# Spreading the FFT units of each batch evenly over its period, with seven products from an earlier group on

## Chip, cores and metric

The kernel runs on one core of a Trainium2 chip. The metric is the device time of one execution in microseconds (us). The kernel before takes 782.4 us (median of the first three executions).

## The reference, cut to what matters

```python
# x: (8, 3008, 256) float32; n_freq = 1505
X = np.fft.rfft(x, axis=1)
y = np.fft.irfft(X * (filt_r + 1j * filt_i)[None], n=3008, axis=1)   # filter along the sequence
x = y.reshape(8 * 3008, 256)
h = np.maximum(x @ w_in, 0.0)                                        # 256 -> 2048
out = h * h @ w_out                                                  # 2048 -> 256
```

Eight batches are filtered, then all 24064 rows go through a feed-forward layer. The kernel overlaps the two: while TensorE works on the feed-forward layer of one batch, the Fourier transform of the next is done in between.

## The kernel before

Time is cut into slots. Group `g` of 512 rows has 8 slots. In each slot TensorE computes two of the 16 hidden blocks of group `g` (L553, four matmuls of 512 columns) and one part of the second layer of group `g-1`. That second layer is either 64 matmuls of 256 columns (L573) or, from group 9 on, seven products of half size (a Strassen-like scheme, 112 matmuls of 128 columns, L666), for which VectorE forms four sums and does three additions.

FFT units of a batch are put between these parts, at "place" 0 (after the first layer's part) or place 1 (after the second layer's) of a slot:

- A, forward: x16 to PSUM, evicted into `u`, which goes to DRAM (`dU`). 16 units.
- read_u: `dU` back as `ut`, 1.5 MB in a different order.
- B, filter: PSUM times the filter on VectorE into `prod`; GpSimd issues two DMAs that add its halves. 12 units.
- P, inverse: from `prod` to PSUM, evicted into `ze`, which goes to DRAM (`dZ`). 12 units.
- read_z: `dZ` back as `zt`. Y, inverse: `zt` to PSUM, evicted into `yt`, the rows of the first layer. 16 units.

All of A, B, P and Y use the same two PSUM banks, and A, Y and P are evicted by ScalarE or VectorE behind whatever else these have in their queues:

```python
def psF(name):
    return pps.tile([128, 512], F32, tag="psF", name=name, bufs=2)
...
def unit_a(b, a):
    ...                                   # one or two matmuls into psF
    if a % 2 == 0: nc.scalar.copy(out=o, in_=pv)
    else:          nc.vector.tensor_copy(out=o, in_=pv)
    if i == 3:     write_u(b, c)          # nc.sync.dma_start
def read_u(b):
    ut = p_ut.tile([128, NC, D], F16, ...)               # one buffer
    for s0, s1 in ((0, 8), (8, 24)):                     # 512 KB, 1024 KB
        nc.sync.dma_start(out=ut[:, s0:s1, :], in_=v[:, s0:s1, :])
def unit_b(b, p):
    ...                                   # two matmuls into psF
    nc.vector.tensor_mul(out=prod, in0=ps..., in1=sF...)
    for i in range(2): nc.gpsimd.dma_start(..., accum_op=add)
def unit_p(b, p):                         # two matmuls into psF, nc.scalar.copy
    ...
def fft_plan(b):                          # r: slot in the batch's frame of 48 slots
    ...
    t0 = 2 if b == 1 else 5
    for a in range(12 if b == 1 else 0, 16): put(t0 + a // 2, a % 2, unit_a, b, a)
    put(10 if b == 1 else 13, 1, read_u, b)
    t0 = 14 if b == 1 else 18
    for p in range(12):
        r = t0 + (15 if b == 1 else 18) * p // 11
        put(r, 0, unit_b, b, p)
        ...
        put(r + 4, 1, unit_p, b, p)
    t0 = 34 if b == 1 else 41
    for c in range(4): put(t0 if c < 3 else t0 + 6, 1, read_z, b, c)
    for n in range(16): put((38 if b == 1 else 45) + n // 2, n % 2, unit_y, b, n)
...
for s in range((NG + 1) * SLOTS):
    g, k = divmod(s, SLOTS)
    ffn_g1(g, k)                          # matmuls, then relu on ScalarE
    run(work, s, 0)                       # FFT units of place 0
    products(...) or ffn_g2(g - 1, k)     # second layer of the group before
    run(work, s, 1)                       # FFT units of place 1
    ffn_out / sums(g - 1, k); ffn_sq(g, k)
```

(The guards on `g` and the prologue, which does batch 0 and half of batch 1, are left out.)

## Time and profile before

| | before |
|---|---|
| time, median of 3 | 782.36 us |
| span of the profiled run | 780.7 us |
| matmuls at their usual pace | 745.7 us |
| holes on TensorE, whole span | 28.2 us |
| of these after 60 us | 18.4 us |

A "hole" here is the time from one matmul's start to the next, less the median of that distance for the first one's shape, where over 0.1 us is left. It is used instead of the idle times in the profile because a matmul's end is modelled there. The prediction below shows the lines of the page, the waits, the windows and the timeline on which this rests, and how each is read.

### The profile page before, as it was taken

The page shows a single profiled execution, that of the slowest core. Times are in us where ns is not written, and L with a number is a line of the kernel's source. Part 1 is how long each engine was busy: PE and PEld are TensorE (multiplying, and loading weights), DVE is VectorE, ACT ScalarE, POOL GpSimd, SP SyncE. Part 2 cuts the span into 40 slices and gives each one's busy share as a digit, 9 for nine tenths or more (in the row PEclk, how much of TensorE's full clock was granted, in tenths as well). Part 3 has the DMA queues.
Part 4 walks back from the last instruction along what each step waited for, and adds up shares of the span by engine and source line. Part 5 has one row for each costly group of instructions (what it writes and reads, how often), then busy time and mean ns, then how long its engine had stood idle before and what let it go on. Part 6 is the DMA issues. An engine that isn't in the chain of part 4 may idle for free. (4 is left out here: it accounts for less than half of the span.)

```text
span 780.7 us, 18857 instructions
## 1 busy us (share of the span) xinstructions
PE 755.4 (97%) x7878; PEld 552.5 (71%) x7878; DVE 627.2 (80%) x699; ACT 561.6 (72%) x785; POOL 193.0 (25%) x260
## 2 busy tenths in 40 slices
PE   8989999999999999999999999999999999999998
PEld 6746667667676676876778767777767767777776
DVE  6856644567778997899978999899988999987874
ACT  3976776767777677776777777776777767777774
POOL 3801730036100561005500065002840035100000
PEclk9999999999999999999999999999999999999999
DMA  9985974369534795167953578525875355521011
GB/s 365 375 253 160 149 161 116 89 158 175 136 80 119 169 171 145 57 180 130 171 116 96 173 127 149 154 76 158 149 145 126 89 151 128 128 78 55 29 55 55
DMA packets 104941, 109.20 MB, mean 140 GB/s; under 512 B 9640, under 2 KB 93096, under 8 KB 102936
## 3 DMA queue, kind: packets, MB, share of 16 engines
q1 hardware_dynamic: 85704, 87.38, 37.3%
q0 software_dynamic: 19008, 20.43, 19.5%
q8 instruction: 62, 1.02, 0.6%
q10 hardware_dynamic: 144, 0.18, 0.1%
q14 instruction: 23, 0.19, 0.1%
HBM read 58.12 MB, written 48.23 MB: 136 GB/s over the span
## 5 line engine op out<-in xcount | busy, mean ns | idle before, releaser
L557 ACT ACTIVATE h<-psH 128x1024 f16<-128x1024 f32 x376 | 384.6, 1024 | 172.2 <-PE psH L553 170.3
L553 PE MATMUL psH<-yt,sWin 128*128 128x512 f16 (+7 forms) x1728 | 386.9, 351 | 1.5 <-DVE yt L532 0.5
L564 DVE TENSOR_TENSOR h<-h 128x2048 f16<-128x2048 f16 (+1 forms) x192 | 229.6, 1196 | 64.8 <-ACT h L557 64.3
L457 POOL DMA_DIRECT2D prod<-prod x168 | 141.1, 997 | 463.7 <-DVE prod L450 458.4
L553 PEld LDWEIGHTS <-sWin 128*128 128x128 f16 x1728 | 153.4, 98 | 98.5 <-issue 3.4
L666 PEld LDWEIGHTS <-sum 128*128 128x128 f16 x2368 | 146.8, 98 | 27.2 <-issue 6.1
L666 PEld LDWEIGHTS <-h 128*128 128x128 f16 x1776 | 110.3, 98 | 22.5
L450 DVE TENSOR_TENSOR prod<-psB,sF 128x1024 f16<-128x1024 f32 x84 | 102.4, 1219 | 14.4 <-PE psB L442 14.4
L666 PE MATMUL psX<-sT,sum 128*128 128x128 f16 x1184 | 84.2, 219 | 0.0
L573 PE MATMUL psO<-sWout,h 128*128 128x256 f16 x640 | 81.8, 272 | 0.0
L573 PEld LDWEIGHTS <-h 128*128 128x128 f16 x640 | 62.0, 98 | 14.6 <-issue 0.2
L532 DVE CAST yt<-psY 128x376 f16<-128x376 f32 x62 | 33.8, 546 | 34.4 <-PE psY L523 34.4
L489 ACT CAST ze<-psP 128x512 f16<-128x512 f32 x84 | 49.4, 588 | 13.4 <-PE psP L487 8.9
L666 PE MATMUL psY<-sT,sum 128*128 128x128 f16 x592 | 57.2, 219 | 0.0
L666 PE MATMUL psY<-sWout,sum 128*128 128x128 f16 x592 | 44.9, 219 | 5.5 <-DVE bot L681 5.5
L364 DVE CAST u<-psA 96x512 f16<-96x512 f32 x50 | 34.1, 683 | 17.1 <-PE psA L358 14.9
L523 PE MATMUL psY<-sC,zt 112*128 112x94 f16 x512 | 42.4, 205 | 5.1 <-DMA zt<-dZ 4.9
L195 POOL DMA_DIRECT2D x<-in_x_dram x40 | 46.1, 1151 | 0.0
L642 DVE TENSOR_TENSOR sum<-sum,h 128x2048 f16<-128x2048 f16 x37 | 45.2, 1221 | 0.9
L666 PE MATMUL psY<-sWout,h 128*128 128x128 f16 x592 | 45.2, 219 | 0.0
L666 PE MATMUL psX<-sT,h 128*128 128x128 f16 x592 | 45.1, 219 | 0.0
L639 DVE TENSOR_TENSOR sum<-h 128x2048 f16<-128x2048 f16 x37 | 44.9, 1215 | 0.1
(88 smaller groups left out, 706.0 us busy)
## 6 DMA issues: line engine op xcount, KB each, us to landing
zt<-dZ SPq DMA_DIRECT2D x64, 192.0 KB
dU<-u SPq DMA_DIRECT2D x28, 384.0 KB
prod<-prod POOLq DMA_DIRECT2D x168, 64.0 KB, 3.6
dZ<-ze SPq DMA_DIRECT2D x28, 384.0 KB
x<-in_x_dram POOLq DMA_DIRECT2D x40, 192.0 KB, 5.3
ut<-dU SPq DMA_DIRECT2D x7, 1024.0 KB
xw<-in_x_dram SPq DMA_DIRECT2D x6, 1024.0 KB
ut<-dU SPq DMA_DIRECT2D x7, 512.0 KB
```

Source lines behind the costliest of these rows:

```text
L195: nc.gpsimd.dma_start(out=t, in_=v[:, m, :])
L450: nc.vector.tensor_mul(out=prod, in0=ps.rearrange("p (a d) -> p a d", d=D).unsqueeze(1).to_broadcast([128, 2, 2, D]), in1=sF[:, :, 2 * p:2 ...
L457: nc.gpsimd.dma_start(out=prod[64 * i:64 * i + 64, 0], in_=prod[64 - 64 * i:128 - 64 * i, 1], accum_op=mybir.AluOpType.add)
L489: nc.scalar.copy(out=zes[(b, c)][:, 2 * i6:2 * i6 + 2, :], in_=ps.rearrange("p (a d) -> p a d", d=D))
L523: nc.tensor.matmul(ps[:, 94 * jj:94 * jj + 94], zt[:, 4 * (g % 2) + jj, dt * 128:(dt + 1) * 128], sSY, start=True, stop=True)
L553: nc.tensor.matmul(ps[:, i, o:o + n], sWin[:, dt, jt * 128:(jt + 1) * 128], yts[b][:, dt, r:r + n], start=(dt == 0), stop=(dt == 1))
L557: nc.scalar.activation(out=h2[:, 2 * s:2 * s + 2, :], in_=ps, func=AF.Relu)
L564: nc.vector.tensor_mul(out=v, in0=v, in1=v)
L573: nc.tensor.matmul(pso[g][:, t % 2, :], h2s[g][:, jt, t * 128:(t + 1) * 128], sWout[:, jt, :], start=(jt == 0), stop=(jt == NJT - 1))
L639: nc.vector.tensor_add(out=t, in0=a21, in1=a22)
L642: nc.vector.tensor_sub(out=t, in0=f[5], in1=a11)
L666: nc.tensor.matmul(o[:, t, :], f[p][:, q, 128 * t:128 * t + 128], sg["w"][p][:, q, :], start=(m == 0 and p in (1, 2)), stop=(q == 7), skip ...
```

## The change

Its intent: take the bursts away. Filter units come every 3.5 slots in place of 1.6, forward units every 2.75 in place of two per slot; the odd forward evictions move from VectorE to ScalarE; the last P unit is two slots earlier so that z has time to come back; and the cheaper seven-product form starts at group 6.

```diff
-    p_prod = ... bufs=4
+    p_prod = ... bufs=5
-        if a % 2 == 0:
+        if a % 2 == 0 or b > 2:
             nc.scalar.copy(out=o, in_=pv)
-    ztiles = [... for c in range(3)]
+    ztiles = [... for c in range(2)]
@@ fft_plan: put(r, f, *a) now takes r in half slots
-        t0 = 2 if b == 1 else 5
-        for a in range(12 if b == 1 else 0, 16):
-            put(t0 + a // 2, a % 2, unit_a, b, a)
-        put(10 if b == 1 else 13, 1, read_u, b)
+        else:
+            for a in range(16):
+                if a % 2 == 0 and b > 2:
+                    put((-57 + 2.3 * a) if b == 3 else (-66 + 2.75 * a), load_x, b, a // 2)
+                put((-16 + a, -46 + 2.2 * a, -56 + 2.75 * a)[min(b, 4) - 2], unit_a, b, a)
+            put(2 if b == 2 else -9, read_u, b)
-            r = t0 + (15 if b == 1 else 18) * p // 11
-            put(r, 0, unit_b, b, p)
-            put(r + 4, 1, unit_p, b, p)
+            r = 14 + 15 * p / 11 if b == 1 else 6 + 28 * p / 11 if b == 2 else -5 + 39 * p / 11
+            put(r, unit_b, b, p)
+            put(r + 4.5, unit_p, b, p)
-        for c in range(4):
-            put(t0 if c < 3 else t0 + 6, 1, read_z, b, c)
-        for n in range(16):
-            put((38 if b == 1 else 45) + n // 2, n % 2, unit_y, b, n)
+        for c in range(4):
+            put((41, 41.5, 48, 54)[c] - d, read_z, b, c)
+        for n in range(16):
+            put(YN[n] - d, unit_y, b, n)
+    YN = (45, 45.5, 46, 46.5, 47.5, 49, 50.5, 52, 54, 56, 58, 60, 63, 66, 69, 72)
-    SEVEN = range(9, NG - 1)
+    SEVEN = range(6, NG - 1)
```

(Cut: the four operand differences of the seven products go to four slots in place of one, and the last read of z of batch 0 is placed later.)

More of the change, by code (lines that the diff above doesn't have):

```diff
@@ L143 @@
     p_ut = ctx.enter_context(tc.tile_pool(name="p_ut", bufs=1))
-    p_prod = ctx.enter_context(tc.tile_pool(name="p_prod", bufs=4))
+    p_prod = ctx.enter_context(tc.tile_pool(name="p_prod", bufs=5))
     p_ze = ctx.enter_context(tc.tile_pool(name="p_ze", bufs=3))
@@ L494, in unit_p @@
                 in_=zes.pop((b, c)))
-    ztiles = [const.tile([112, 8, D], F16, name=f"zt_{c}") for c in range(3)]
+    ztiles = [const.tile([112, 8, D], F16, name=f"zt_{c}") for c in range(2)]
     for t in ztiles:
@@ L501, in read_z @@
     def read_z(b, c, ks=(0, 1)):
-        zt = ztiles[c % 3]
+        zt = ztiles[c % 2]
         v = dZ[b].rearrange("(q j) d -> q j d", j=NM)
@@ L609, with make_t @@
     sg = {}
-    def make_t():
-        t = p_t.tile([128, 4, 8, 128], F16, tag="t", name="sT")
+    def make_t(k):
         w = sWout.rearrange("p (q e) c -> p q e c", e=2)
@@ L616, in make_t @@
         b21, b22 = w[:, :, 1, 0:128], w[:, :, 1, 128:256]
-        nc.vector.tensor_sub(out=t[:, 0], in0=b12, in1=b11)
-        nc.vector.tensor_sub(out=t[:, 1], in0=b22, in1=t[:, 0])
-        nc.vector.tensor_sub(out=t[:, 2], in0=b22, in1=b12)
-        nc.vector.tensor_sub(out=t[:, 3], in0=b21, in1=t[:, 1])
+        if k == 0:
+            sg["t"] = p_t.tile([128, 4, 8, 128], F16, tag="t", name="sT")
+        t = sg["t"]
+        i0, i1 = ((b12, b11), (b22, t[:, 0]), (b22, b12), (b21, t[:, 1]))[k]
+        nc.vector.tensor_sub(out=t[:, k], in0=i0, in1=i1)
         sg["w"] = {1: b11, 2: b21, 3: b22, 4: t[:, 3], 5: t[:, 0], 6: t[:, 1], 7: t[:, 2]}
@@ L692, in fft_plan, with put @@
         plan = {}
-        def put(r, place, f, *a):
-            plan.setdefault((r, place), []).append((f, a))
+        def put(r, f, *a):
+            r = int(2 * r)
+            plan.setdefault(divmod(r, 2), []).append((f, a))
+        d = 0
         if b == 1:
             for n in range(4, 16):
-                put(n if n < 8 else n + 2 if n < 12 else 2 * n - 7, n % 2, unit_y, 0, n)
+                put((n if n < 8 else n + 2 if n < 12 else 2 * n - 7) + n % 2 / 2, unit_y, 0, n)
+            put(7.5, read_z, 0, 3)
             for k in range(4):
-                put((4, 5, 7, 7)[k], 1, cast_wout, k, nc.vector)
-        t0 = 2 if b == 1 else 5
-        for a in range(12 if b == 1 else 0, 16):
-            put(t0 + a // 2, a % 2, unit_a, b, a)
-        put(10 if b == 1 else 13, 1, read_u, b)
-        t0 = 14 if b == 1 else 18
-        for p in range(12):
-            r = t0 + (15 if b == 1 else 18) * p // 11
-            put(r, 0, unit_b, b, p)
-            if b + 1 < B and 2 <= p < 10:
-                put(r, 0, load_x, b + 1, p - 2)
-            put(r + 4, 1, unit_p, b, p)
-        t0 = 34 if b == 1 else 41
+                put((4.5, 5.5, 7.5, 7.5)[k], cast_wout, k, nc.vector)
+            for a in range(12, 16):
+                put(2 + a / 2, unit_a, b, a)
+            put(10.5, read_u, b)
+            d = 7
+        else:
[4 more added lines that the diff above has]
+            put(2 if b == 2 else -9, read_u, b)
+        for p in range(12):
+            r = 14 + 15 * p / 11 if b == 1 else 6 + 28 * p / 11 if b == 2 else -5 + 39 * p / 11
+            put(r, unit_b, b, p)
+            if b == 1 and 2 <= p < 10:
+                put(r, load_x, 2, p - 2)
+            put(r + 4.5, unit_p, b, p)
         for c in range(4):
-            put(t0 if c < 3 else t0 + 6, 1, read_z, b, c)
+            put((41, 41.5, 48, 54)[c] - d, read_z, b, c)
         for n in range(16):
-            put((38 if b == 1 else 45) + n // 2, n % 2, unit_y, b, n)
+            put(YN[n] - d, unit_y, b, n)
         return plan
+    YN = (45, 45.5, 46, 46.5, 47.5, 49, 50.5, 52, 54, 56, 58, 60, 63, 66, 69, 72)
     def run(plan, r, place):
@@ L791 @@
     prologue[0] = False
-    for c in range(2, 4):
-        read_z(0, c)
-    SEVEN = range(9, NG - 1)
+    read_z(0, 2)
+    SEVEN = range(6, NG - 1)
     work = {}
@@ L806 @@
         run(work, s, 0)
-        if s == SEVEN[0] * SLOTS:
-            make_t()
+        if SEVEN[0] * SLOTS <= s < SEVEN[0] * SLOTS + 4:
+            make_t(s % SLOTS)
         if (s - 1) // SLOTS - 1 in SEVEN:
```

## The prediction

> **What bounds the kernel now.** I read the page first, then the waits, then the batches window by window, then the timeline at the holes.
>
> ```profile
> span 780.7 us, 18857 instructions
> ...
> PE 755.4 (97%) x7878; PEld 552.5 (71%) x7878; DVE 627.2 (80%) x699; ACT 561.6 (72%) x785; POOL 193.0 (25%) x260
> ...
> DVE  6856644567778997899978999899988999987874
> ```
>
> TensorE is the bound, and its clock row is full throughout. VectorE averages 80% but has slices at 9: its bursts. The page overstates PE, because a matmul's end is modelled. So I took start-to-start times from the timeline: the usual pace is 0.216 us for 512 columns, 0.109 for 256, 0.056 for 128, 0.041 for a 94-column inverse matmul. All matmuls at these paces come to 745.7 us; what exceeds a pace by over 0.1 us I call a hole. Holes sum to 28.2 us, of which 18.4 lie after 60 us (the rest is the prologue and the first slots, which the change hardly touches). These 18.4 us are all that a reordering can win.
>
> Who ends them, in the waits view:
>
> ```profile
> PE psY L666 <- DVE bot L681: 5.5, 5, 1.2
> PE psY L523 <- DMA zt<-dZ: 4.9, 7, 1.4
> ...
> PE psP L487 <- DMA prod<-prod: 2.6, 4, 0.7
> ```
>
> These are idle times counted from the modelled ends, so they are low. By my starts, after 60 us: accumulator additions by VectorE 6.8 us (a hole of 1.3 to 1.4 and one of 0.12 in each of five batches); z arriving late 4.4 (six holes, 0.37 to 1.06); products of the inverse arriving late, late in the burst, 4.1; u arriving late 0.8; waits for a psF bank 1.6; others 0.7. The batches repeat:
>
> ```profile
> core 0: us, PE busy (x) PEld busy (x) DVE busy (x) ACT busy (x) POOL busy (x), PEclk, DMA share, GB/s
> ...
> 308.30:402.30 94.00, 91.14 (x1026) 68.08 (x1024) 84.09 (x95) 69.16 (x100) 24.07 (x32) 1.00 0.61 137
> ...
> 717.66:730.82 13.16, 13.16 (x147) 9.39 (x145) 10.45 (x12) 9.35 (x12) 0.00 (x0) 1.00 0.13 41
> ```
>
> A batch takes 94.0 us, 90.5 of it matmuls at pace; the tail's groups, with no FFT beside them, run without a hole at 13.16 us. The largest hole, as timeline:
>
> ```profile
> 264.04 0.39 PE L666 MATMUL psY<-sWout,h 128*128 128x128 f16 x4
> ...
> 264.61 1.21 DVE L564 TENSOR_TENSOR h<-h 128x2048 f16<-128x2048 f16 x1
> ...
> 265.74 1.21 DVE L450 TENSOR_TENSOR prod<-psB,sF 128x1024 f16<-128x1024 f32 x1
> ...
> 266.88 0.41 DVE L681 TENSOR_TENSOR top<-psY,top 128x256 f32<-128x256 f32 x1
> ...
> 267.21 0.41 DVE L681 TENSOR_TENSOR bot<-psY,bot 128x256 f32<-128x256 f32 x1
> ...
> 267.67 0.38 PE L666 MATMUL psY<-sWout,sum 128*128 128x128 f16 x4 [1.24 <-DVE bot L681]
> ```
>
> The addition's input is complete at 264.3, but VectorE first works off a square and a filter product queued ahead, and TensorE stands until the addition has read the bank. This is burst damage: filter units every 1.6 slots.
>
> **What the Trainium skill says.** "TensorE: Matmul & The Clock Gate", "Wait — 56ns, not 53.3ns?", puts a warm matmul at N/2.4 GHz plus about 2.5 ns; the chain's 16 matmuls of 128 columns in 0.89 us (0.0556 each) agree. The same page, "Back-to-back issue gap", gives about 81 ns for N=128 with a weight load each; this trace has a weight load each and holds 0.056, so the measurement decides (with 81 the seven-product form would lose). "PSUM — Partial Sum Buffer", "Engine vs sequencer instructions", says the ScalarE and VectorE queues are strict FIFO; the fence above is that. "VectorE: DVE Perf Modes", "The perf-mode tier table", gives 1224 ns for a 2048-element bf16 tensor_tensor and the slowest mode with a PSUM operand: here 1.196 us for 2048 and 1.219 us for 1024 from PSUM.
>
> **The change part by part.**
> 1. Seven products from group 6 instead of 9: three groups trade 64 matmuls of 256 columns (8 in 0.88 us, so about 7.0) for 112 of 128 columns (112 x 0.056 = 6.3). 0.7 to 0.8 us each, on the path: -2.3 us. VectorE gets 3 x (4 x 1.216 + 3 x 0.417) = +18.3 us, at 150 to 200 us where it was half idle. The four operand differences (0.68 us each) go to four slots.
> 2. The odd forward evictions of batches 3 to 7 go to ScalarE: 40 x 0.683 = -27.3 us of VectorE, 40 x 0.573 = +22.9 us of ScalarE. Totals: VectorE about 618, ScalarE about 586. Neither becomes the bound on average.
> 3. Filter units now every 3.5 slots in place of 1.6, with no forward evictions on VectorE. In the burst VectorE had 11.0 (four squares, four sums, three additions) / 8 + 1.22 / 1.64 = 2.1 us per slot against some 1.9 of TensorE; now 1.37 + 0.34 = 1.7. The addition holes should go: -6.4 of 6.8. The fifth product buffer and the quieter GpSimd queue should remove the late products, -4.0.
> 4. The last inverse-side product moves from slot 40.5 of the batch's frame to 38.5 while z is still used at 45. Each earlier slot is 1.9 us, the largest hole 1.06: -3.4 for batches 2 to 7 (batch 1 keeps its distance and its 1.0). u is read 4 slots ahead, but its writes now end before the read instead of just ahead of it: -0.7.
> Sum of 3 and 4: -14.5. No matmul is added.
>
> **What comes back.** All FFT units share two psF banks, so a unit waits for the eviction of the unit two before it. Before, dense phases had one unit per half slot, ScalarE and VectorE taking turns, and lost nothing to speak of. Where three units fell within half a slot the trace shows a price:
>
> ```profile
> 136.50 1.02 ACT L557 ACTIVATE h<-psH 128x1024 f16<-128x1024 f32 x1 [0.70 <-PE psH L553]
> ...
> 137.42 0.47 ACT L530 CAST yt<-psY 128x376 f16<-128x376 f32 x1
> ...
> 137.94 0.33 PE L523 MATMUL psY<-sC,zt 112*128 112x94 f16 x4 [0.21 <-ACT yt L530]
> ```
>
> The eviction stands behind the 1.02 us relu: 0.38 us lost by starts, then 0.32 by the next unit, and 0.44 twice (84 and 93 us) behind a filter product. Listing both plans by slot and half slot, the old has 8 such triples, the new 45, because four streams (forward A, filter B, inverse P, inverse Y) of different spacing now cross: 20 in slots 19 to 71, where batches 1 to 3 meet, six in each of the next four batch frames, one in the last. Worst is three at one place (P, B, A in slot 29): the third wants a bank whose eviction has not begun: relu 0.92 + copy 0.58 less 0.22 of matmuls, some 1.2 us. Working through the triples with 0.92 us of relu, 0.35 to 0.58 of copy, 1.22 of filter product: about 7 us in the early stretch (1.6 of it existed), 1.5 in each of four batches, 0.6 in the last; 12 more than before. Stalls let the evictors catch up, so one prevents the next: I take 9.
>
> Net: -2.3 - 14.5 + 9.0 = -7.8 us. 782.4 - 7.8 = **774.6 us**.
>
> **Rivals.** (a) Spreading works as meant: ScalarE's slack within a slot (1.02 of relu in 1.9) absorbs the crossings. For: Y and A ran at two units a slot before without loss, and the spacings look hand-picked. New holes 2 to 3 us: about 768. (b) The two banks become the wait in place of the additions, at full count or more, because a filter product on VectorE holds a bank until the sums ahead of it are done: 14 to 16 us of new holes, 780 to 782. For: the measured 0.3 to 0.4 per triple and strict FIFO. Against: the old triples on ScalarE alone often cost nothing. (c) VectorE stays the bound locally, where sevens, filter units and inverse evictions now coincide (150 to 200 us: about 1.9 us a slot against 1.95): addition holes of about 1 us survive in group 6 to 9, 1 to 3 us on top of any of these. (d) Transfers: DMA share falls in the peaks (0.97 to 0.99 before) as traffic spreads; I expect no new wait on one.
>
> **Range and chances.** With no hole left at all after 60 us: 782.4 - 2.3 - 18.4 = 761.7, a floor. (a) at 768 and (b) at 781 bound the likely outcomes: low 765.5, high 780.5. Faster by over 2% needs under 766.7, more than (a) delivers: 0.12. Slower needs new holes of over 30 us: 0.01. Within 2%: 0.87.
>
> **What would show it.** Right: the wait of TensorE for the bottom addition falls from 5.5 us to under 1; waits for z from 4.9 to about 2.5 (the prologue's and batch 1's remain); for products to under 1; VectorE's digits in the middle are flatter. New rows should be waits of forward, filter and inverse matmuls on ScalarE's u, ze, yt copies and on the filter product, 8 to 12 us together by starts, most before 200 us. Batches 4 to 6 should take 91.5 to 92.5 us in place of 94. Wrong: a batch still at 93.5 or more, holes ended by a transfer, or ScalarE's relus late so that the first layer's matmuls wait (0.5 us before).

## More of the kernel before

Unless a run is called slow, every number here is from executions in the fast state. The sets ran on several chips; each ratio is to the kernel before in the same set, and holes are read from one profiled execution per version.

## The result, and the profile after

The changed kernel takes 787.16 us (785.37 to 787.64, 4 runs) against 783.03 us of the kernel before in the same rounds. The ratio is 1.0052, with a 95% interval of 1.0027 to 1.0077: slower by half a per cent. (All ratios are the mean time of one kernel's fast runs over that of the other's of the same rounds, so not quite the ratio of the medians quoted.)

The page of the changed kernel, in the rows that answer to those shown in the prediction:

```profile
span 785.6 us, 19161 instructions
...
PE 756.2 (96%) x8022; PEld 554.5 (71%) x8022; DVE 619.7 (79%) x679; ACT 583.7 (74%) x831; POOL 192.7 (25%) x260
...
DVE  5866655579768988888987899779987999878874
```

VectorE and ScalarE moved as intended (627.2 to 619.7 and 561.6 to 583.7 us), and VectorE's row has fewer nines. Yet the span grew by 4.9 us. The waits of TensorE:

```profile
PE psY L523 <- DMA zt<-dZ: 6.8, 4, 2.5
...
PE psP L487 <- DVE prod L450: 3.0, 7, 0.5
...
PE psA L358 <- DVE prod L450: 2.8, 11, 0.3
...
PE psY L523 <- ACT h L557: 2.3, 2, 1.2
...
PE psA L358 <- ACT ze L489: 1.5, 2, 1.1
```

The columns are total, times and longest. The wait for the bottom addition (5.5 us before) and the one for a product's DMA (2.6) are gone from the list. The wait for z has grown from 4.9 to 6.8, with a longest of 2.5 in place of 1.4, and A and P units now wait for evictions. By starts, after 60 us, and by what the stopped unit needed:

| holes after 60 us, us | before | after |
|---|---|---|
| bottom addition (L681) late | 6.9 | 0 |
| product of B late for P | 4.1 | 0 |
| u late for B | 0.8 | 0 |
| z late for the first Y | 4.5 | 8.9 |
| psF bank not yet evicted | 1.6 | 14.5 |
| others | 0.5 | 0.8 |
| sum | 18.3 | 24.2 |

(The sum before is 18.35, hence 18.3 here and 18.4 above.) With this, the 4.9 us are accounted for: matmuls at pace 745.7 to 743.6, that is -2.1; holes after 60 us +5.9; excesses of under 0.1 us from 0.5 to 1.8, that is +1.3; prologue -0.2. Two new losses thus have to be explained, z and psF.

**The z holes.** One stretch around the largest, from the timeline of the changed kernel, of SyncE's queue (SPq: start and duration of the issues) and of the units concerned:

```profile
211.08 0.58 ACT L489 CAST ze<-psP 128x512 f16<-128x512 f32 x1
...
211.69 0.38 SPq L492 DMA_DIRECT2D dZ<-ze  x1
...
212.18 1.83 SPq L433 DMA_DIRECT2D ut<-dU  x2
...
214.11 1.65 SPq L606 DMA_DIRECT2D out_dram<-bot  x3
...
215.86 1.34 SPq L606 DMA_DIRECT2D out_dram<-top  x3
...
218.22 3.77 SPq L505 DMA_DIRECT2D zt<-dZ  x4
...
224.81 0.47 PE L523 MATMUL psY<-sC,zt 112*128 112x94 f16 x4 [2.52 <-DMA zt<-dZ]
```

The last P unit is evicted at 211.7, so the intended lead is there. But right behind its write to DRAM stands the read of u, 1.5 MB, for the next batch. The read of z is issued at 218.2 only. The list of SyncE's waits has the reason:

```profile
SPq L505 <- DMA ut<-dU: 11.7, 7, 2.3
```

L505 is the read of z. In the program's order a transfer waits for the one eight before it on this queue (they share a completion semaphore), and in batch 2 that is the read of u. In batches 3 to 6 the two reads that the first Y needs did not wait for u; the next two did, and the other waits of the line are theirs. There z's first reads were issued in time but did not move in time: in batch 3 the first was issued at 311.8, but in the trace's list of packets the 4096-byte packets of z begin at 316.5, after u's and behind the stores issued between (in the four batches 4.2 to 4.8 us after the issue); the matmul starts at 319.7. So both kinds of waiting are there: for the completion of u once, for its bytes in the queue four times. In the kernel before, u is read at slot 13 of the frame and z at 41, so they never meet. Batches 2 to 6 have such holes (2.7, 1.3, 1.6, 1.3 and 2.0 us). Batch 7, after which no u is read, has none.

The 2.7 us hole also costs clock. Windows of the changed kernel around it (PEclk is the granted clock, the share of full speed that TensorE was given):

```profile
core 0: us, PE busy (x) PEld busy (x) DVE busy (x) ACT busy (x) POOL busy (x), PEclk, DMA share, GB/s
...
223.00:225.00 2.00, 0.19 (x3) 0.22 (x4) 0.00 (x0) 0.35 (x1) 0.09 (x1) 0.87 1.13 213
225.00:226.00 1.00, 1.00 (x13) 1.00 (x11) 0.00 (x0) 0.47 (x1) 0.00 (x0) 0.50 1.21 168
226.00:227.00 1.00, 1.00 (x12) 1.00 (x10) 0.00 (x0) 0.00 (x0) 0.00 (x0) 0.50 0.45 86
227.00:228.00 1.00, 1.00 (x8) 0.62 (x7) 0.44 (x1) 0.39 (x2) 0.00 (x0) 0.56 0.02 4
```

For some 3 us TensorE runs at half pace (the trace's record of the clock has 0.5 from 224.5 to 227.9). After 60 us, the traces have such a stretch in four versions, each at a hole of 2.1 us or more or within 1.2 us of its end (2.1, 2.5, 2.7 and 4.3 us), and at no hole of up to 2.0 us. The +1.3 us of small excesses fit that: matmuls of 128 columns at twice 0.056 us stay under the 0.1 us from which I count a hole.

**The psF holes.** One of the worst, from the timeline of the changed kernel at slot 29, where P, B and A stand at one place:

```profile
107.43 0.38 PE L487 MATMUL psP<-prod,sSP 128*128 128x256 f16 x2
107.63 1.02 ACT L557 ACTIVATE h<-psH 128x1024 f16<-128x1024 f32 x1 [0.59 <-PE psH L553]
107.65 0.38 PE L442 MATMUL psB<-ut,sSB 128*128 128x256 f16 x2
...
108.56 0.58 ACT L489 CAST ze<-psP 128x512 f16<-128x512 f32 x1
...
109.19 0.38 PE L358 MATMUL psA<-x,sC 94*96 94x512 f16 x1 [1.15 <-ACT ze L489]
```

P takes one bank, B the other, and A wants P's bank at 107.9. ScalarE first does the slot's relu, then evicts P at 108.6 to 109.1. TensorE stands 1.3 us by starts.

### The profile page after: what moved, and what is told of

The parts are those of the page before. It is cut to its first block, busy times and chain, and to the rows that moved or that the text cites.

```text
span 785.6 us, 19161 instructions
## 1 busy us (share of the span) xinstructions
PE 756.2 (96%) x8022; PEld 554.5 (71%) x8022; DVE 619.7 (79%) x679; ACT 583.7 (74%) x831; POOL 192.7 (25%) x260
## 4 chain that ended last, share of the span: by engine, by line
PE 82%; DMA 7%; DVE 6%; ACT 2%; issue 1%; SPq 1%; DVEq 0%; ACTq 0%
PE psH L553 36%; PE psX L666 17%; PE psY L666 12%; PE psO L573 6%; DVE prod L450 3%; PE psA L358 3%; PE psP L487 2%; PE psY L523 2%; DMA zt<-dZ 2%; PE psB L442 2%; DMA f<-in_filt_i_dram 2%; ACT h L557 1%; DVE h L564 1%; DMA ut<-dU 1%; DVE sum L639 1%
## 5 line engine op out<-in xcount | busy, mean ns | idle before, releaser
L666 PEld LDWEIGHTS <-sum 128*128 128x128 f16 x2560 | 158.9, 98 | 25.2 <-issue 1.4
L666 PEld LDWEIGHTS <-h 128*128 128x128 f16 x1920 | 119.1, 98 | 20.5 <-issue 1.4
L666 PE MATMUL psX<-sT,sum 128*128 128x128 f16 x1280 | 91.9, 220 | 0.0
L666 PE MATMUL psY<-sT,sum 128*128 128x128 f16 x640 | 62.0, 219 | 0.0
L573 PE MATMUL psO<-sWout,h 128*128 128x256 f16 x448 | 56.9, 272 | 0.0
L523 PEld LDWEIGHTS <-zt 112*128 112x128 f16 x512 | 34.3, 98 | 29.1 <-issue 10.4
L362 ACT CAST u<-psA 96x512 f16<-96x512 f32 x90 | 52.3, 581 | 2.8 <-PE psA L358 2.2
L573 PEld LDWEIGHTS <-h 128*128 128x128 f16 x448 | 43.2, 98 | 14.8 <-issue 4.5
L642 DVE TENSOR_TENSOR sum<-sum,h 128x2048 f16<-128x2048 f16 x40 | 48.9, 1222 | 0.9
L648 DVE TENSOR_TENSOR sum<-h,sum 128x2048 f16<-128x2048 f16 x40 | 48.7, 1216 | 0.0
L639 DVE TENSOR_TENSOR sum<-h 128x2048 f16<-128x2048 f16 x40 | 48.6, 1216 | 0.0
```

The source lines that it names most:

```text
L523: nc.tensor.matmul(ps[:, 94 * jj:94 * jj + 94], zt[:, 4 * (g % 2) + jj, dt * 128:(dt + 1) * 128], sSY, start=True, stop=True)
L573: nc.tensor.matmul(pso[g][:, t % 2, :], h2s[g][:, jt, t * 128:(t + 1) * 128], sWout[:, jt, :], start=(jt == 0), stop=(jt == NJT - 1))
L639: nc.vector.tensor_add(out=t, in0=a21, in1=a22)
L642: nc.vector.tensor_sub(out=t, in0=f[5], in1=a11)
L666: nc.tensor.matmul(o[:, t, :], f[p][:, q, 128 * t:128 * t + 128], sg["w"][p][:, q, :], start=(m == 0 and p in (1, 2)), stop=(q == 7), skip ...
```

## The experiments

Four questions: are the psF triples the cause of the psF holes; is the read of u the cause of the z holes; what is each remaining part of the change worth; and do the cures add up?

### Seven products alone

The kernel before with `SEVEN = range(6, NG - 1)` and the operand differences spread over four slots.

> The kernel before with only the seven products from group 6 (and the four operand differences in four slots). By pace 3 x (64 x 0.109 - 112 x 0.056) = 2.1 us less, about 781 if VectorE has room in groups 6 to 8. If VectorE's 18 us of added sums between 150 and 200 us make new holes, 783 or more.

Measured: 782.14 us, ratio 1.000 (0.998 to 1.002). The 2.1 us of pace are there (743.6), but holes on the bottom addition went from 6.9 to 8.9 us, and one product came 1.8 us late at 199 us. A new addition hole of 1.4 us stands at 172.6 us, so in the bursts of the old plan VectorE had no room for 18 us more in groups 6 to 8. In this trace holes after 60 us grew by 1.0 us in all, half of the gain; the times of the set show none of it, within some 1.6 us.

### No three psF users within a slot

```diff
+    # no three units of the two psF banks within one slot: Y and A units step aside
+    for fs in ((unit_b, unit_p), (unit_y,), (unit_a,)):
+        ...
+                while count.get(t, 0) + max(count.get(t - 1, 0), count.get(t + 1, 0)) > 1:
+                    t += 1      # half a slot later
```

B and P stay where the changed kernel has them. No matmul, eviction or transfer is added or taken away.

> The changed kernel with forward and inverse units moved by half slots, most by 0.5 to 1.5 and in batch 2 up to 5, so that no three units that use the two psF banks fall within one slot; nothing else. Theory B (the triples make the new holes, each third unit waiting for an eviction behind a relu or a filter product): psF holes fall from about 14.5 us to under 4, time 10 us less, about 777. Rival V (those holes come from VectorE and ScalarE being too full on average once three groups more use sevens and ScalarE has all forward evictions): moving units by half slots keeps over 10 us of them, time over 784. The z holes (8.9 us) stay.

Measured: 774.23 us, ratio 0.9905 (0.9877 to 0.9933); 787.16 to 774.23 is 13 us (the two sets ran apart; by their ratios it is 11.5). psF holes fell from 14.5 to 0.8 us and z holes stayed at 8.2. So the engines were not too full: the crossings of the four streams made the holes.

### The read of u earlier

```diff
-            put(2 if b == 2 else -9, read_u, b)
+            put(2 if b == 2 else -11.5, read_u, b)
```

> The changed kernel with one edit: from batch 3 on the read of u is put 2.5 slots earlier (at -11.5 in place of -9), so that its 1.5 MB are through before z is read. Theory Q (the read of u for the next batch now stands just ahead of the read of z in the same DMA queue and holds it back): the five z holes of batches 2 to 6 (8.9 us by starts in the changed kernel) shrink to under 3 us in all, time 6 us less than the changed kernel, about 781. Rival T (z is late because its own write to DRAM and read back are slow however early they are issued): holes stay within 1 us of 8.9, time unchanged at 787. The psF holes (14 us) stay in both.

Measured: 792.91 us (787.92 to 794.86), ratio 1.0121 (1.0092 to 1.0150): the expected time was wrong. The z holes did shrink, from 8.9 to 1.3 us, as theory Q wants. But u now meets the last product of the batch. The timeline of this run:

```profile
579.28 1.64 POOL L457 DMA_DIRECT2D prod<-prod  x2 [6.33 <-DVE prod L450]
...
579.84 0.81 SPq L433 DMA_DIRECT2D ut<-dU  x2
...
588.75 0.61 PE L487 MATMUL psP<-prod,sSP 128*128 128x256 f16 x2 [4.14 <-DMA prod<-prod]
```

GpSimd issues the two DMAs that add the halves of the product just as u's read begins. The second took 8.9 us to land, against a median of 2.8. Holes on products came to 7.4 us in four batches, where there were none. The profiled run is the fastest of the six (787.9), so the others lost more than its trace shows; their granted clocks are 0.989 to 0.998, where it has 0.998 with one stretch of half clock behind the 4.3 us hole. The wait had only moved.

### The read of u through another queue

```diff
-            nc.sync.dma_start(out=ut[:, s0:s1, :], in_=v[:, s0:s1, :])
+            (nc.gpsimd if b > 2 else nc.sync).dma_start(out=ut[:, s0:s1, :], in_=v[:, s0:s1, :])
```

> The changed kernel with one edit: from batch 3 on the same read of u, at the same place, is issued by GpSimd's queue in place of SyncE's. The bytes in flight are the same; only the order within SyncE's queue changes, where a transfer waits for the one eight before it. Theory Q1 (it is the place in the queue: z's read is issued only when u's read, 8 or 9 issues before, has landed): z holes fall from 8.9 to under 3 us, time about 781. Theory Q2 (it is the bandwidth that 1.5 MB of u take while z is read): z holes stay over 6 us, time within 2 us of 787.

Measured: 780.05 us, ratio 0.9972 (0.9955 to 0.9988). z holes 1.7 us, psF holes 15.1 as before. That agrees with Q1 in the numbers, but the run does not separate Q1 from Q2. GpSimd's queue was not held up by the write of z, so u's read began at 300.5 in batch 3, 4.6 us ahead of that write in place of 0.5 us behind it, and its last packet had ended (309.4) when z was read (309.6). One product came 0.5 us late. What it shows is that z is in time once u is not in front of it.

### u in pieces on the same queue

(Shortened.)

```diff
-                put(-9, read_u, b)                       # 512 KB and 1024 KB
+                for k in range(4):
+                    put(-9 + 10.5 * k, read_u, b, k)     # 384 KB each, 3 filter units' worth
```

> The changed kernel with one edit: from batch 3 on u is read in four pieces of 384 KB, 10.5 slots apart, on SyncE's queue as before, the first at the same place. Theory Q (1.5 MB of u between z's write and z's read hold up the queue and the DMA engines): z holes fall from 8.9 to under 3 us and no product is late (unlike with the earlier read), time about 780. If any read of u ahead of z in the same queue is enough, holes stay over 5 us, time 784 or more.

Measured: 778.72 us, ratio 0.9917 (0.9892 to 0.9942). No z hole is left, no product is late, and psF holes are at 15.7. The waits of z's read for u's, 11.7 us before, are down to:

```profile
SPq L506 <- DMA ut<-dU: 0.6, 1, 0.6
```

(One line was added above, so L505 is L506 here.) Same queue, same place, a quarter of the bytes in front: it is the amount that stands ahead of z. In batch 3, where z's first two reads wait for no u in either version, its packets now begin 2.0 us after the first issue (309.1 to 311.0) in place of 4.8. In batch 2 the one issue fewer also takes z's first read off u's semaphore. Whether 1.5 MB on a separate queue at the very same time would do no harm stays open.

### Both cures, two ways

The same two edits together, with u on GpSimd's queue, and with u in pieces.

> Both cures at once: no three users of the psF banks within a slot, and from batch 3 on u is read through GpSimd's queue. If the two causes are separate their gains add: the de-tripled kernel ran at 774.2 with about 8.2 us of z holes left, the other queue removed about 7 of 8.9. Expected 767 to 768, ratio to the kernel before about 0.98. If removing one only uncovers the other (the holes hide behind each other), 772 or more.

> No three users of the psF banks within a slot, and u in four pieces on SyncE's queue: 767 to 768 if the pieces do as well as the other queue; 774 if they do nothing.

Measured: 768.64 us with the other queue, ratio 0.9791 (0.9763 to 0.9819), about as expected; 763.56 us with pieces, ratio 0.9728 (0.9700 to 0.9755), some 4 us better than expected. With the other queue, holes of 2.0 on z and 1.8 on a late product remained; with pieces, holes after 60 us come to 1.6 us in all. A batch in the version with pieces, to be held against the 91.14 of the kernel before in the same window:

```profile
308.30:402.30 94.00, 94.00 (x1070) 70.92 (x1069) 82.85 (x92) 75.90 (x113) 24.15 (x32) 1.00 0.62 137
```

TensorE is busy for all of it, and does 1070 matmuls in place of 1026. This version beats both kernels. A second run of it, for the comparison below:

> The version with pieces and no triples once more, on the same chip as the late-product kernel, for a direct comparison: 763 to 764, no hole on z after 60 us.

Measured: 763.48 us, ratio 0.9763 (0.9742 to 0.9784); no hole on z after 60 us.

One thing has to be known before differences of 2 us are read. Within the fast state, executions of the versions with pieces with a granted clock of 0.998 tend to take 1 to 2.5 us longer than those at 0.999 or 1.0: here 765.9 against 763.2 to 763.7. Where such an execution was profiled, its trace has one stretch of 3.4 us at half clock, near 49 us, in the prologue. So like is compared with like below.

### What the other parts are worth, with the two faults gone

*Forward evictions back on VectorE* (`if a % 2 == 0:`), first on the version with the other queue, then on the one with pieces:

> The kernel with both cures, with one part of the change undone: the odd forward evictions of batches 3 to 7 go back to VectorE (27 us more there, 23 us less on ScalarE). If VectorE had to be relieved for the additions to be on time: holes ended by the bottom addition come back (over 3 us), time 3 us or more above the version with both cures. If the even spacing of the filter units alone did it: within 1.5 us of it.

> The version with pieces and no triples (763.6 us, 1.6 us of holes after 60 us), with the odd forward evictions of batches 3 to 7 back on VectorE. The same test on the other-queue version cost 3.3 us, but in holes for z, a late product and triples, with no late addition. If the move to ScalarE is what frees the additions: 3 us or more slower with holes on the bottom addition. If the even spacing of the filter units alone did that: no such hole, within 3 us, what is lost being psF holes of 0.4 each.

Measured: 771.96 us (768.64 with the move), so neither expected outcome came: it was 3.3 us slower, but with no hole on the bottom addition. Over half of its added holes were on z (5.9 in place of 2.0), which the move should not touch and which stay unexplained, so I repeated it on the version with pieces: 765.28 us, ratio 0.9759 (0.9739 to 0.9778), that is 1.7 us slower than 763.56. That set ran on another chip; the four-buffer version below, on the same one, took 763.72. In neither is there one hole on the bottom addition. So the new spacing of the units freed the additions without the move; the move to ScalarE is worth some 1.6 us, and psF holes of 0.42 in each of four batches, 1.7 us, account for it.

*Seven products from group 9 again:*

> The version with pieces and no triples, with seven products only from group 9 again. Alone on the kernel before, the earlier start gained nothing (1.000), because new holes on additions and products ate its 2.1 us. With the holes gone its full 2.1 us should show: 765.7. If it gains nothing here either: 763.6.

Measured: 765.92 us, ratio 0.9770 (0.9749 to 0.9792), 2.4 us slower; at a clock of 1.0, 765.4 against 763.1 to 763.8, some 2 us. The same edit that gained nothing on the kernel before is worth its full pace once nothing else stops TensorE.

*Four product buffers in place of five:*

> The version with pieces and no triples, with four product buffers in place of five. Filter units come every 3.5 slots and each product is used 4.5 slots later, so two are live at once: I expect no difference in batches 3 to 7, and at most 1 us in batch 1, where they come every 1.36 slots. If the fifth buffer is what ended the late products: 2 us or more slower.

Measured: 763.72 us, ratio 0.9742 (0.9721 to 0.9762): no difference. With this spacing the fifth buffer is not what ends the late products. (Nor do the two z buffers, cut from three, hurt: the versions with pieces have two and no hole on z.)

*P two slots later, so that z is read half a slot behind the last one:*

```diff
-            put(r + 4.5, unit_p, b, p)
+            put(r + (6.5 if b > 1 else 4.5), unit_p, b, p)
```

> The version with pieces and no triples, with the inverse products of batches 2 to 7 two slots later (6.5 slots after their filter unit, the last at 40.5 as in the kernel before), so that z is read half a slot behind the last one in place of 2.5. If the lag removed the z holes of the kernel before (4.4 us): 3 to 5 us slower, with holes of 0.4 to 1.1 us on z. If without u in the way z is early enough anyhow: within 1 us.

> The late-product kernel once more, unchanged: its profiled execution fell in a state in which TensorE ran at a quarter of its pace throughout, so that its holes could not be read. Timed runs gave 765.2 to 767: I expect 766 to 767 and 2 to 4 us of holes that z ends, 0.3 to 0.9 each in batches 2 to 7. If no such holes are there, the lag is not what costs the 3 us.

Measured first: 765.24 to 767.24 us in the four fast runs, their median 766.1, ratio 0.9770. The profiled run took 2788 us and is a slow one: TensorE took 0.84 us for 512 columns where 0.216 is usual, all through. Its holes say nothing. Run again: 765.52 us, ratio 0.9788 (0.9768 to 0.9807) against 763.48 us and 0.9763 for the version with pieces on the same chip. The two intervals overlap, but at a clock of 0.999 or more it is 765.4 to 765.5 against 763.2 to 763.7: some 2 us. The trace has four z holes (0.8, 0.2, 0.6 and 0.7), 2.3 us in all; six, in batches 2 to 7, were expected. So the lag of two slots does remove z holes, as predicted, where u is not in the way, but about half of the 4.4 us that the prediction had seen.

Holes after 60 us in the versions that carry the argument, by starts:

| us | after | no triples | u in pieces | both |
|---|---|---|---|---|
| z | 8.9 | 8.2 | 0 | 0 |
| psF | 14.5 | 0.8 | 15.7 | 1.1 |
| others | 0.8 | 1.0 | 0.6 | 0.5 |
| time, median | 787.2 | 774.2 | 778.7 | 763.6 |

## Why the prediction was wrong

It forecast 774.6 us with a range of 765.5 to 780.5; measured were 787.16. By the spans it said -7.8 us and +4.9 came. Step by step:

1. *Seven products, -2.3.* Pace -2.1, which is also what its own figures give (three groups of 64 x 0.109 less 112 x 0.056): right. Rival (c), that VectorE would hold this up around groups 6 to 9, came true on the kernel before (ratio 1.000), but not in the changed one, which has no hole on an addition.
2. *Evictions to ScalarE.* Totals of 618 and 586 us were forecast, 619.7 and 583.7 measured: right.
3. *Additions -6.4, products -4.0.* Measured -6.9 and -4.1: right, and the mechanism too, though the prediction credited three edits together. The spacing does it; the moved evictions are worth some 1.6 us elsewhere and the fifth buffer nothing.
4. *z, -3.4.* This is the step that failed. "The last inverse-side product moves from slot 40.5 of the batch's frame to 38.5 while z is still used at 45" is true, and worth some 2 us when alone (the late-product run). But z holes grew by 4.4 us. I gave u's read its own line ("its writes now end before the read instead of just ahead of it: -0.7", measured -0.8) and looked only at what it waits for. I did not lay the next batch's frame over this one: slot -9 of one is slot 39 of the other, between the last write of z and its read at 41. Rival (d), "I expect no new wait" on a transfer, fell with it. Off by 7.8 us. The change of clock after the longest hole was in no step: about 1.3 us.
5. *What comes back, +9.* The mechanism was right, the size not. Working through the 45 triples gave 12 us more than before; then I took 9, because "stalls let the evictors catch up, so one prevents the next". Measured +12.9. The trace bore the count out (7 us forecast for the early stretch; the same three holes of 0.64, 0.38 and 0.44 us return in four batches) and gave no ground for the discount. Off by 3.9 us. Rival (b), the full count or more, described this part; its 14 to 16 us were a little high.

The forecast and the measured difference of the spans lie 12.7 us apart. The two misses (7.8 and 3.9) and the clock (1.3) come to 13.0; small terms of the other sign make up the difference. Two of the prediction's own signs of being wrong came: holes ended by a transfer, and batches still at 93.5 us or more (93.8, 93.5 and 93.7 between the first Y matmuls of batches 3 to 6).

Slips besides: the prediction gave batch 1 a z hole of 1.0. The hole at 214 us belongs to batch 2; batch 1 had none. "A hole of 1.3 to 1.4 ... in each of five batches" is 0.87 in one of them. And 1.196 us for 2048 elements on VectorE mixes two shapes; 128x2048 alone takes 1.218. None of the three changes the sum by much.

## What to carry to other kernels

Spreading work evenly within each stream is half the task: where several streams share a pair of PSUM banks or one DMA queue, list who meets whom, across the frames of neighbouring batches too, and move units by half a slot until no three meet. A large read that is needed piece by piece is worth issuing piece by piece; moved earlier as a whole, it met another victim here. And an edit that gains nothing while other stalls stand, as the seven products did, may be worth its full price once they are gone.

## What the Trainium skill lacked or had wrong

- "TensorE: Matmul & The Clock Gate", "Back-to-back issue gap", gives about 81 ns per matmul of N=128 in a stream of weight loads and matmuls. Here such a stream holds 56 ns (16 in 0.89 us), in every trace but the slow one.
- The same page, "HAM oscillation — how this bites in real kernels", states as the rule no idle gaps over some 3.4 us. Here a gap of 2.5 us was followed by about 3 us at a granted clock of 0.50 to 0.56, and in another version so was a hole of 2.1 us. No smaller bound is shown: near 49 us four traces have such a stretch with no hole over 1.7 us before it.
- "DMA: Bandwidth & Descriptors", "Queues, rings and completion order", says that on each engine descriptors are consumed in ring order. This case agrees, and the page would have warned of step 4: z's packets began at 316.5 us, though issued at 311.8, behind u's 1.5 MB. It does not say what follows for a schedule; here a 1.5 MB read in front cost up to 2.7 us of TensorE, and 384 KB none.
- The TensorE page, "Seeing it yourself", mentions a clock gate seen stuck at a quarter for over 50 us, but no page that I found gives a cause. In one execution here matmuls of 512 columns took 0.84 us, 3.9 times the usual 0.216, throughout (2788 us in all); its page prints a clock of 1.000, but its trace holds no record of the clock. It is one run of over seventy, and nothing here explains it or shows that it is the same thing.
